# Linear attention and a snake MLP on one core: second products and attention rearranged in the first three tiles

## The chip, the core and the metric

The kernel runs on one NeuronCore of a Trainium2 chip. Five engines work side by side, each with its own queue of instructions taken in order: TensorE (PE, matrix products into the accumulation memory PSUM), VectorE (DVE), ScalarE (ACT), GpSimd (POOL) and SyncE (SP, which here issues the transfers). The metric is the device time of one execution in microseconds (us), as the median of several runs.

## The reference

```python
def _attn_ref(q, k, v):                 # 8 batches, 8 heads, 576 positions, 64 columns
    q_s = np.exp(q - max over the 64);  q_s = q_s / sum over the 64
    k_s = np.exp(k - max over the 576); k_s = k_s / sum over the 576
    kv = np.einsum('bhsd,bhse->bhde', k_s, v)
    return np.einsum('bhsd,bhde->bhse', q_s, kv)

def _moe_ref(x, w_in, w_out, alpha):    # x: 4608 x 512, w_in: 512 x 2048, w_out: 2048 x 512
    h = x @ w_in
    s = np.sin(alpha * h)
    g = h + s * s / (alpha + 1e-09)
    return g @ w_out
```

`x` is the attention's output with the heads side by side. All inputs and the output are float32.

## The kernel before

**Attention, per batch.** `load` brings q, k and v of one batch (1152 KB each) into staging buffers, six of which are shared with the weights (1 MB each). `exp_q` and `exp_k` take exponentials on ACT, in halves. `norm_q` sums q's exponentials over the 64 columns on DVE (L145), takes reciprocals (L146) and multiplies (L147) on the engines it is given. `cast_v` (L131) makes v bfloat16, beside a column of ones, so that the product of k and v (`kv_mm`, 36 small products into `kvp`, L156) also gives k's sums. `kv_norm` divides by these sums into `kvb` (L167, L168). `q_transpose` turns the normalised q in two groups (12 and 6 transposes into `tp`, L183) with a copy each to `qT` (L184). `attn_out` makes four groups of products `xp` (L196), each copied to `xT` (L199), the transposed bfloat16 input of the second part. All of this shares one PSUM buffer (`ps_a`, two banks), so each product waits for the copy before it.

**The MLP, in nine tiles of 512 rows.** A tile has 16 steps: `mm_h` makes 128 columns of h with four products of 512 columns (L209), `sine` takes the sine on ACT (L215) and squares it on ACT (L217), POOL (L219) or DVE (L221), `combine` makes one slice of g on DVE (L225). The string `SQ0` or `SQ1` says which engine squares in which step of tiles 0 and 1; later tiles square on ACT. The second product, `mm_o` (L229), takes 64 products per tile, 16 for each of four output blocks. `evac_o` (L234) copies a block out of PSUM into one of three buffers `o` and issues two transfers. h has four PSUM banks (`ps_h`), the blocks have two (`ps_o`).

**The order.** It is written out by hand: the order of the calls is the order on every engine. Batch 0's attention comes first, under transfers of the weights, which POOL casts to bfloat16 (L254, L257). Tile 0 then makes all of its h, then all four blocks of its second product at once (two in `ps_o`, two in `ps_h`), then attention 1 by itself. Tile t (from 1) makes its h with the second products of tile t-1 between its steps (none in tile 1), and holds attention t+1: the exponentials after step 0, kv at step 4, the transposes at 6 and 7, the products `xp` at 8 to 11. On SP's queue all transfers stand in the order of the calls.

ACT has one set of function tables active at a time: before an exponential that follows a sine, and a sine that follows an exponential, stands a table load.

Of the kernel before, what the change touches and what calls it, by code (L numbers as in the profile page):

```python
# [23 lines left out]
def kernel(  # L24
# [35 lines left out]
    spool = ctx.enter_context(tc.tile_pool(name="spool", bufs=3))  # L60
# [41 lines left out]
    def load_win(c):  # L102
        st = stage.tile([128, 4, 512], F32, name="st_w", tag="st")
        nc.sync.dma_start(out=st, in_=win_v[:, :, c * 512:(c + 1) * 512])
        wst["i", c] = st
# [55 lines left out]
    def kv_norm(b):  # L161
        A["kvb", b] = kt = att2.tile([128, 2, 2, D], BF16, name="kvb")
        kvr = small.tile([128, 2, 2], F32, name="kvr")
        for x in range(2):
            r = slice(64 * x, 64 * x + 64)
            src = A["kvp", b][r, :, 0:260].rearrange("p e (ii c) -> p e ii c", ii=2)
            nc.vector.reciprocal(kvr[r], src[:, :, :, x * 65 + 64])  # L167
            nc.vector.tensor_tensor(kt[r], src[:, :, :, x * 65:x * 65 + 64],  # L168
                                    kvr[r].unsqueeze(3).to_broadcast([64, 2, 2, D]), op=ALU.mult)
# [75 lines left out]
    load("v", v, 0, halves=True)  # L245
    for c in range(4):
        load_win(c)
    make_identity(nc, ident)
    DVE_CP(identb, ident)
    for n in range(2):  # L250
        nc.vector.memset(vb[n].rearrange("p j (i c) -> p j i c", i=4)[:, :, :, D:D + 1], 1.0)

    def cast_win(c, eng):
        eng(win[:, :, c * 512:(c + 1) * 512], wst["i", c])  # L254
# [4 lines left out]
    with tc.tile_pool(name="ps_s", bufs=4, space=PSUM) as ps_s:  # L259
# [16 lines left out]
        cast_win(0, POOL_CP)  # L276
# [3 lines left out]
        load_batch(1)  # L280
# [18 lines left out]
    combine(0, *pend)
    cast_wout(2, POOL_CP)  # L300
# [107 lines left out]
```

## Time and profile before

| | |
|---|---|
| median of three runs | 339.1 us (338.93 to 339.96) |
| the profiled execution | 340.48 us, its span 338.7 us |
| PE busy | 291.6 us (86%) |
| ACT busy | 237.5 us (70%) |
| DVE busy | 200.6 us (59%) |
| POOL busy | 71.7 us (21%) |

The span runs from the first to the last instruction that the profiler saw. A busy PE is not PE at its peak, since products overlap and their ends are modelled. The granted clock of TensorE is given as a share of full speed: 1.00 is 2.4 GHz, 0.50 is 1.2 GHz, and a number between is a mean over a stretch. The name in brackets behind an idle time is what ended it.

### The profile page before, as it was taken

The numbers are of one execution on the slowest core, as the hardware profiler recorded it, in microseconds if no ns is written. First come the engines' busy times: TensorE is split into PE (matmuls) and PEld (weight loads), VectorE is DVE, ScalarE is ACT, GpSimd is POOL, SyncE is SP. The second block draws the span as 40 slices with busy tenths as digits, with TensorE's granted clock in tenths as the row PEclk, the third lists the DMA queues.
The fourth block names the chain that finished last, engine by engine and source line by source line (L and its number), as shares of the span: only waits on it lengthen the run. The fifth ranks groups of instructions, "written<-read, shape, count | busy, mean of one in ns | idle before, by whom it ended". The sixth has DMA issues, their size and how long they took to land.

```text
span 338.7 us, 4528 instructions
## 1 busy us (share of the span) xinstructions
PE 291.6 (86%) x1713; PEld 134.9 (40%) x1713; DVE 200.6 (59%) x286; ACT 237.5 (70%) x328; POOL 71.7 (21%) x47
## 2 busy tenths in 40 slices
PE   0585895484799899989998999899989999999994
PEld 0432342322334444443444445444534444444441
DVE  3648761206886786487558755874687545555511
ACT  4476862268479867986897789778968777777600
POOL 0456632026443700150024003300400000000000
PEclk9979999556999999999999999999999999999999
DMA  7999903999500111850195029302111111211132
GB/s 266 389 386 387 391 10 76 309 392 391 215 0 0 33 31 33 297 199 19 38 333 173 3 62 362 120 4 59 33 31 31 32 31 33 50 44 33 32 93 62
DMA packets 22758, 46.44 MB, mean 137 GB/s; under 512 B 1728, under 2 KB 1744, under 8 KB 22736
## 3 DMA queue, kind: packets, MB, share of 16 engines
q1 hardware_dynamic: 22736, 46.15, 41.4%
q8 instruction: 13, 0.21, 0.3%
q14 instruction: 9, 0.07, 0.1%
HBM read 36.71 MB, written 9.44 MB: 136 GB/s over the span
## 4 chain that ended last, share of the span: by engine, by line
PE 49%; ACT 21%; DVE 18%; issue 6%; POOL 2%; DMA 2%; SPq 0%; ACTq 0%; POOLq 0%
PE op L229 22%; PE hp L209 20%; ACT s L215 7%; DVE g L225 7%; ACT ke L117 3%; ACT qe L117 3%; ACT L215 2%; ACT L117 2%; ACT s L217 2%; PE xp L196 2%; DVE kvb L168 2%; PE hp L229 2%; DVE s L221 2%; DVE qT L184 2%; PE tp L183 2%
## 5 line engine op out<-in xcount | busy, mean ns | idle before, releaser
L209 PE MATMUL hp<-xT,win 128*128 128x512 bf16 x576 | 150.5, 389 | 12.4 <-DVE g L225 11.4
L225 DVE SCALAR_TENSOR_TENSOR g<-s,inva_sb,hp 128x512 bf16<-128x512 f32 x144 | 105.9, 744 | 70.4 <-ACT s L217 65.2
L229 PE MATMUL op<-wout,g 128*128 128x512 bf16 x544 | 138.6, 380 | 0.0
L215 ACT ACTIVATE s<-hp,alpha_sb 128x512 f32<-128x512 f32 x144 | 97.8, 683 | 49.7 <-PE hp L209 36.8
L209 PEld LDWEIGHTS <-win 128*128 128x128 bf16 x576 | 56.8, 100 | 84.5 <-issue 21.4
L217 ACT ACTIVATE s<-s 128x512 f32<-128x512 f32 x126 | 79.4, 630 | 4.0
L229 PEld LDWEIGHTS <-g 128*128 128x128 bf16 x576 | 53.8, 98 | 63.4 <-issue 0.5
L147 POOL TENSOR_TENSOR qn<-qe,qs 128x2304 bf16<-128x2304 bf16 (+1 forms) x7 | 26.7, 3817 | 115.2 <-PE hp L209 100.7
L145 DVE TENSOR_REDUCE qs<-qe 128x36 f32<-128x2304 bf16 (+1 forms) x10 | 20.7, 2071 | 27.2 <-ACT qe L117 27.2
L234 DVE COPY o<-op 128x512 f32<-128x512 f32 x33 | 22.3, 676 | 14.0 <-PE op L229 14.0
L183 PE MATMUL tp<-identb,qn 128*128 128x128 bf16 x144 | 11.9, 234 | 20.9 <-DVE qn L147 9.2
L199 DVE CAST xT<-xp 128x512 bf16<-128x512 f32 (+1 forms) x28 | 20.8, 745 | 5.5 <-PE xp L196 5.5
L219 POOL TENSOR_TENSOR s<-s 128x512 f32<-128x512 f32 x12 | 12.9, 1076 | 39.4 <-ACT s L215 39.4
L183 PEld LDWEIGHTS <-qn 128*128 128x128 bf16 x144 | 9.8, 104 | 26.7 <-issue 16.3
L117 ACT ACTIVATE qe<-st_q 128x1152 bf16<-128x1152 f32 x16 | 17.8, 1156 | 3.4 <-DMA st_q<-in_q_dram 3.4
L131 POOL CAST vb<-st_v 128x1152 bf16<-128x1152 f32 x14 | 16.9, 1236 | 15.2 <-DMA st_v<-in_v_dram 15.2
L117 ACT ACTIVATE ke<-st_k 128x1152 bf16<-128x1152 f32 x16 | 17.7, 1149 | 0.7 <-DMA st_k<-in_k_dram 0.7
L196 PE MATMUL xp<-qT,kvb 64*64 64x256 bf16 (+1 forms) x128 | 10.4, 320 | 5.4 <-DVE kvb L168 2.5
L156 PE MATMUL kvp<-vb,ke 64*128 64x130 bf16 x288 | 12.4, 252 | 0.9 <-ACT qT L184 0.9
L156 PEld LDWEIGHTS <-ke 64*128 64x128 bf16 x288 | 10.8, 112 | 4.2 <-ACT s L215 3.0
L215 ACT ACT_TABLE_LOAD x8 | 10.3, 1283 | 1.7 <-PE hp L209 1.6
L117 ACT ACT_TABLE_LOAD x8 | 10.3, 1283 | 0.9 <-PEq L392 0.7
(28 smaller groups left out, 75.8 us busy)
## 6 DMA issues: line engine op xcount, KB each, us to landing
out_dram<-o SPq DMA_DIRECT2D x72, 128.0 KB, 2.4
st_q<-in_q_dram SPq DMA_DIRECT2D x7, 1152.0 KB, 6.3
st_k<-in_k_dram SPq DMA_DIRECT2D x7, 1152.0 KB, 9.6
st_v<-in_v_dram SPq DMA_DIRECT2D x7, 1152.0 KB, 11.1
st_w<-in_moe_w_in_dram SPq DMA_DIRECT2D x4, 1024.0 KB, 13.6
st_w<-in_moe_w_out_dram SPq DMA_DIRECT2D x4, 1024.0 KB, 15.7
st_q<-in_q_dram SPq DMA_DIRECT2D x2, 576.0 KB, 4.3
st_k<-in_k_dram SPq DMA_DIRECT2D x2, 576.0 KB, 6.4
```

Source lines behind the costliest of these rows:

```text
L117: nc.scalar.activation(dst[:, :, ii * 128:(ii + 1) * 128].rearrange("p j (x d) -> p x j d", x=2), src[:, ii::2], AX.Exp)
L145: nc.vector.tensor_reduce(part, src, axis=AXL.X, op=ALU.add)
L147: engs[h].tensor_tensor(dst, src, part.unsqueeze(3).to_broadcast([128, J, w, D]), op=ALU.mult)
L156: nc.tensor.matmul(kvp[:, e, ii * 130:(ii + 1) * 130], ke[r, j, ii * 128:(ii + 1) * 128], vt[r, j, ii * 130:(ii + 1) * 130], start=(j == 0 ...
L183: nc.tensor.transpose(tp[:, h, 2 * jj + ii], qn[:, j, ii * 128:(ii + 1) * 128], identb)
L199: eng(xT[:, ii::2, c0:c0 + n], xp[:, :, 0:n])
L209: nc.tensor.matmul(hp, win[:, ki, ni * 128:(ni + 1) * 128], xT[:, ki, t * MF:(t + 1) * MF], start=(ki == 0), stop=(ki == 3))
L215: nc.scalar.activation(s, hp, AX.Sin, scale=alpha_sb[:, ni:ni + 1])
L217: nc.scalar.activation(s, s, AX.Square)
L225: nc.vector.scalar_tensor_tensor(G[t][:, ni], in0=s, scalar=inva_sb[:, ni:ni + 1], in1=hp, op0=ALU.mult, op1=ALU.add)
L229: nc.tensor.matmul(acc, G[t][:, ni, j * 128:(j + 1) * 128], wout[:, ni, :], start=(ni == 0), stop=(ni == nN - 1))
L234: eng(o, acc)
```

## The change

The order of the first three tiles is rewritten.

- Front: the first half of q of batch 0 is normalised on POOL, v is cast on DVE, 14 products on data without use run on PE ahead of the transposes, a sine of one element loads its table ahead of tile 0, and the first quarter of w_in comes and is cast in two parts. All loads up to batch 2 are issued here, in the order weights, batch 1, batch 2; before, batch 2 came after tile 0's outputs.
- Tile 0: the squares go round ACT, DVE and POOL; h uses six PSUM banks (four of `ps_h` and two of `ps_o`); POOL's casts of the weights stand at other steps.
- Its second product is made in two pairs of blocks, with attention 1 between the products of the second pair.
- Tile 1 makes its h with no attention in it, then 50 of its 64 second products, with attention 2 between them. Tile 2 makes its h with the 14 products that are left and with attention 3 (exponentials after step 2, kv at step 7, the rest at 9 to 15), and squares on POOL and ACT in turn.
- From tile 3 on the order is as before, except that kv is at step 5, the transposes at 7 and 9, and `xp` at 10 to 13.
- `kv_norm` takes one reciprocal for both halves; the last evacuation is split over DVE and ACT, and its second transfer is issued on ACT's queue; the sines have four buffers instead of three.

```diff
-    spool = ctx.enter_context(tc.tile_pool(name="spool", bufs=3))
+    spool = ctx.enter_context(tc.tile_pool(name="spool", bufs=4))
...
-        kvr = small.tile([128, 2, 2], F32, name="kvr")
+        kvr = small.tile([128, 2, 2, 2], F32, name="kvr")
+        src = A["kvp", b][:, :, 0:260].rearrange("p e (ii x c) -> p e ii x c", ii=2, x=2)
+        nc.vector.reciprocal(kvr, src[:, :, :, :, D])
...
+        if wide and ni % 6 >= 4:
+            hp = ps_o.tile([128, MF], F32, name="op", tag="o")
+        else:
+            hp = ps_h.tile([128, MF], F32, name="hp", tag="h")
...
+        if last:
+            nc.vector.tensor_copy(o[:, 0:dm // 2], acc[:, 0:dm // 2])
+            nc.scalar.copy(o[:, dm // 2:], acc[:, dm // 2:])
+        else:
+            eng(o, acc)
...
+            q_eng = nc.scalar if last and hf else nc.sync
...
+    load_win(0, parts=2)
+    for c in range(1, 4):
+        load_win(c)
     for c in range(4):
-        load_win(c)
+        load_wout(c)
+    load("q", q, 1)
+    load("k", k, 1)
+    load("v", v, 1, halves=True)
+    load_batch(2)
...
-        norm_q(0, [V, V])
-        cast_v(0, [GP, V])
-        for c in range(4):
-            load_wout(c)
+
+        warm = ps_s.tile([128, 4, 128], F32, name="warm", tag="a")
+        for n in range(14):
+            nc.tensor.matmul(warm, identb, A["qe", 0][:, 0:4, 0:128], start=True, stop=True)
+        norm_q(0, [GP, V])
+        cast_v(0, [V, V])
         for g in range(2):
-            q_transpose(0, g, ps_s, ACT_CP)
+            q_transpose(0, g, ps_s, (ACT_CP, ACT_CP)[g])
+        nc.scalar.activation(zero, zero, AX.Sin)
...
+    SQ0 = "ADPADPADPADPADPA"
     for ni in range(nN):
+        h_slot(0, ni, SQ0[ni], lag, wide=True)
+        flush(lag, 1)
+        if ni in (0, 2, 5):
+            cast_win((0, 2, 5).index(ni) + 1, POOL_CP)
+        elif ni in (8, 11, 14):
+            cast_wout((8, 11, 14).index(ni), POOL_CP)
+    flush(lag, 0)
     cast_wout(3, POOL_CP)
...
+    def o_pair(t, j0, pool):
+        tag = "o" if pool is ps_o else "h"
+        accs = [pool.tile([128, dm], F32, name=tag + "p", tag=tag) for _ in range(2)]
+        for ni in range(nN):
+            for n in range(2):
+                mm_o(t, j0 + n, ni, accs[n])
+                yield
+        for n in range(2):
+            evac_o(t, j0 + n, accs[n], (DVE_CP, ACT_CP)[n])
+            if n == 0:
+                yield
...
     exp_q(1)
-    norm_q(1, [V, GP])
+    norm_q(1, [GP, V])
+    os = o_pair(0, 0, ps_o)
+    take(os)
     exp_k(1)
-    cast_v(1, [V, GP])
+    cast_v(1, [GP, V])
+    os = o_pair(0, 2, ps_h)
+    take(os, 16)
+    q_transpose(1, 0, ps_a, ACT_CP)
+    take(os, 2)
+    q_transpose(1, 1, ps_a, ACT_CP)
+    take(os, 2)
     kv_mm(1, 0, ps_a)
     kv_mm(1, 1, ps_a)
     kv_norm(1)
+    take(os, 6)
     for ii in range(2):
         attn_out(1, ii, 0, ps_a, DVE_CP)
+        take(os, 2)
         attn_out(1, ii, 1, ps_a, ACT_CP)
+        take(os, 1)
+    take(os)
+
+    SQ1 = "PAPDPAPAPPDPAPAP"
+    for ni in range(nN):
+        h_slot(1, ni, SQ1[ni], lag, wide=True)
+        flush(lag, 1)
+    flush(lag, 0)
...
+    attn_front(2, [V, GP])
+    os = o_stream(1)
+    take(os, 32)
+    kv_mm(2, 0, ps_a)
+    kv_mm(2, 1, ps_a)
+    kv_norm(2)
+    take(os, 4)
+    q_transpose(2, 0, ps_a, DVE_CP)
+    take(os, 3)
+    q_transpose(2, 1, ps_a, DVE_CP)
+    take(os, 3)
+    for n in range(4):
+        attn_out(2, n // 2, n % 2, ps_a, (DVE_CP, ACT_CP)[n % 2])
+        take(os, 2)
...
+    SQ2 = "PAPAPAPAPAPAPAPA"
+    for ni in range(nN):
+        hp = h_slot(2, ni, SQ2[ni], lag)
+        flush(lag, 1)
+        if ni == 2:
+            flush(lag, 0)
+            attn_front(3, [GP])
+            take(os)
+        attn_back(3, ni - 7)
+    flush(lag, 0)
+
+    for t in range(3, nT):
...
+            if b is not None:
+                attn_back(b, ni - 5)
```

`h_slot` calls `mm_h` and `sine` and puts the step on a list; `flush` calls `combine` for all but the given number of steps on the list. `take(os, n)` issues the next n second products. `attn_front` calls `exp_q`, `exp_k`, `cast_v`, `norm_q` and the next batch's loads; `attn_back(b, n)` does kv at n = 0, the transposes at 2 and 4, and one `attn_out` each at 5 to 8.

## Rows read from the trace of the kernel before

**Rows 1.** Table of stretches: us; busy us and instructions by engine, PEclk, DMA share, GB/s

```profile
54.50:70.24 15.74, 6.33 (x73) 4.00 (x72) 3.63 (x8) 4.67 (x6) 0.00 (x0) 0.60 0.86 269
70.24:98.56 28.32, 20.66 (x125) 9.14 (x125) 18.53 (x27) 18.66 (x23) 13.34 (x10) 0.80 0.71 264
...
131.40:164.20 32.80, 31.59 (x200) 14.52 (x199) 22.35 (x33) 27.34 (x39) 6.32 (x3) 1.00 0.43 141
```

**Rows 2.** The page, DMA traffic in 40 slices of 8.47 us

```profile
GB/s 266 389 386 387 391 10 76 309 392 391 215 0 0 33 31 33 297 199 19 38 333 173 3 62 362 120 4 59 33 31 31 32 31 33 50 44 33 32 93 62
```

**Rows 3.** Groups by line and shape: busy us, mean ns of one, idle before and releaser

```profile
L225 DVE SCALAR_TENSOR_TENSOR g<-s,inva_sb,hp 128x512 bf16<-128x512 f32 x144 | 105.9, 744 | 70.4 <-ACT s L217 65.2 <-POOL s L219 4.9
...
L215 ACT ACTIVATE s<-hp,alpha_sb 128x512 f32<-128x512 f32 x144 | 97.8, 683 | 49.7 <-PE hp L209 36.8 <-DVE g L225 8.8 <-DVE kvr L167 3.0
L217 ACT ACTIVATE s<-s 128x512 f32<-128x512 f32 x126 | 79.4, 630 | 4.0
...
L117 ACT ACTIVATE ke<-st_k 128x1152 bf16<-128x1152 f32 x16 | 17.7, 1149 | 0.7 <-DMA st_k<-in_k_dram 0.7
...
L219 POOL TENSOR_TENSOR s<-s 128x512 f32<-128x512 f32 x12 | 12.9, 1076 | 39.4 <-ACT s L215 39.4
...
L117 ACT ACT_TABLE_LOAD x8 | 10.3, 1283 | 0.9 <-PEq L392 0.7
...
L147 POOL TENSOR_TENSOR qn<-qe,qs 128x1152 bf16<-128x1152 bf16 x1 | 2.4, 2418 | 5.4 <-DVE qs L146 5.4
```

**Rows 4.** Timeline of the front and of tile 0: start us, us, engine, line, idle before

```profile
6.24 1.35 DVE L145 TENSOR_REDUCE qs<-qe 128x18 f32<-128x1152 bf16 x1 [2.96 <-ACT qe L117]
...
10.88 1.36 DVE L147 TENSOR_TENSOR qn<-qe,qs 128x1152 bf16<-128x1152 bf16 x1
...
14.22 2.13 PE L156 MATMUL kvp<-vb,ke 64*128 64x130 bf16 x36
...
18.97 0.38 PE L209 MATMUL hp<-xT,win 128*128 128x512 bf16 x1 [0.54 <-ACT xT L199]
...
20.83 0.69 ACT L215 ACTIVATE s<-hp,alpha_sb 128x512 f32<-128x512 f32 x1
...
30.71 1.89 POOL L257 CAST wout<-st_w 128x2048 bf16<-128x2048 f32 x1
...
31.94 1.21 DVE L221 TENSOR_TENSOR s<-s 128x512 f32<-128x512 f32 x1 [0.39 <-ACT s L215]
```

**Rows 5.** Timeline of attention 1 and the start of tile 1

```profile
58.54 1.45 ACT L184 COPY qT<-tp 128x1536 bf16<-128x1536 bf16 x1
...
70.24 5.63 PE L209 MATMUL hp<-xT,win 128*128 128x512 bf16 x15 [0.25 <-ACT xT L199]
...
80.89 1.86 PE L209 MATMUL hp<-xT,win 128*128 128x512 bf16 x4 [5.02 <-DVE g L225]
```

**Rows 6.** Timeline of the start of tile 2, and of tile 3

```profile
98.56 2.75 PE L209 MATMUL hp<-xT,win 128*128 128x512 bf16 x12 [0.48 <-DVE g L225]
...
133.48 1.03 PE L209 MATMUL hp<-xT,win 128*128 128x512 bf16 x4
...
135.14 1.11 SPq L237 DMA_DIRECT2D out_dram<-o  x2
...
143.93 1.20 PE L156 MATMUL kvp<-vb,ke 64*128 64x130 bf16 x36
...
144.22 0.75 DVE L225 SCALAR_TENSOR_TENSOR g<-s,inva_sb,hp 128x512 bf16<-128x512 f32 x1 [1.26 <-ACT s L217]
...
148.78 0.83 PE L183 MATMUL tp<-identb,qn 128*128 128x128 bf16 x12 [0.74 <-DVE kvb L168]
...
151.59 0.49 PE L183 MATMUL tp<-identb,qn 128*128 128x128 bf16 x6 [0.47 <-DVE qT L184]
```

**Rows 7.** Timeline of the end

```profile
319.09 14.84 PE L229 MATMUL op<-wout,g 128*128 128x512 bf16 x68
...
333.97 0.69 DVE L234 COPY o<-op 128x512 f32<-128x512 f32 x1 [2.76 <-PE op L229]
```

More of the change, by code (lines that the diff above doesn't have):

```diff
@@ L100, with load_win @@
     wst = {}
-    def load_win(c):
+    def load_win(c, parts=1):
         st = stage.tile([128, 4, 512], F32, name="st_w", tag="st")
-        nc.sync.dma_start(out=st, in_=win_v[:, :, c * 512:(c + 1) * 512])
+        n = 4 // parts
+        for h in range(parts):
+            nc.sync.dma_start(out=st[:, h * n:(h + 1) * n], in_=win_v[:, h * n:(h + 1) * n, c * 512:(c + 1) * 512])
         wst["i", c] = st
@@ L275 @@
         kv_norm(0)
-        cast_win(0, POOL_CP)
+        cast_win(0, POOL_CP, parts=2)
         for ii in range(2):
@@ L301, with h_slot, flush @@
-    cast_wout(3, POOL_CP)
-    accs = [ps_o.tile([128, dm], F32, name="op", tag="o") for _ in range(2)]
-    accs += [ps_h.tile([128, dm], F32, name="hp", tag="h") for _ in range(2)]
-    for ni in range(nN):
-        for j in range(4):
-            mm_o(0, j, ni, accs[j])
+    def h_slot(t, ni, sq, lag, wide=False):
+        hp = mm_h(t, ni, wide)
+        s = sine(t, ni, hp, sq)
+        lag.append((t, ni, hp, s))
+        return lag
+    def flush(lag, keep):
+        while len(lag) > keep:
+            combine(*lag.pop(0))
@@ new lines @@
+    lag = []
+    SQ0 = "ADPADPADPADPADPA"
+    for ni in range(nN):
+        h_slot(0, ni, SQ0[ni], lag, wide=True)
[5 more added lines that the diff above has]
+    flush(lag, 0)
+    cast_wout(3, POOL_CP)
+    def o_pair(t, j0, pool):
[9 more added lines that the diff above has]
+                yield
@@ L308, with take @@
+    def take(it, n=None):
+        for _ in iter(int, 1) if n is None else range(n):
+            if next(it, 0) == 0:
+                return
     exp_q(1)
-    norm_q(1, [V, GP])
+    norm_q(1, [GP, V])
+    os = o_pair(0, 0, ps_o)
+    take(os)
     exp_k(1)
-    cast_v(1, [V, GP])
-    for j in range(4):
-        evac_o(0, j, accs[j], ACT_CP if j % 2 else DVE_CP)
-    load_batch(2)
-    for g in range(2):
-        q_transpose(1, g, ps_a, ACT_CP)
+    cast_v(1, [GP, V])
+    os = o_pair(0, 2, ps_h)
@@ L330, in o_stream, with attn_front, attn_back @@
                 if ni == nN - 1:
-                    evac_o(t, j, acc, DVE_CP)
+                    evac_o(t, j, acc, DVE_CP, last=(t == nT - 1 and j == 3))
                 yield
-    SQ1 = "PAPDPAPDPAPDPAPA"
-    for t in range(1, nT):
+    def attn_front(b, engs):
+        exp_q(b)
+        exp_k(b)
+        cast_v(b, [GP, GP])
+        norm_q(b, engs)
+        if b + 1 < B:
+            load_batch(b + 1)
+    attn_front(2, [V, GP])
[12 more added lines that the diff above has]
+        take(os, 2)
+    def attn_back(b, n):
+        if n == 0:
+            kv_mm(b, 0, ps_a)
+            kv_mm(b, 1, ps_a)
+            kv_norm(b)
+        elif n in (2, 4):
+            q_transpose(b, n // 2 - 1, ps_a, DVE_CP)
+        elif 5 <= n < 9:
+            attn_out(b, (n - 5) // 2, (n - 5) % 2, ps_a, DVE_CP)
+    SQ2 = "PAPAPAPAPAPAPAPA"
[9 more added lines that the diff above has]
+    for t in range(3, nT):
         b = t + 1 if t + 1 < B else None
-        os = o_stream(t - 1) if t > 1 else None
+        os = o_stream(t - 1)
         done = 0
-        pend = None
         for ni in range(nN):
@@ L342 @@
             if b is not None:
[L343 to L377 removed]
+                attn_back(b, ni - 5)
+            s = sine(t, ni, hp, "A")
+            combine(t, ni, hp, s)
+            if b is not None and ni == 0:
+                attn_front(b, [GP])
+            want = 20 + 11 * ni // 4 if b is not None else 4 * (ni + 1)
+            take(os, min(64, want) - done)
+            done = min(64, want)
+        take(os)
+    take(o_stream(nT - 1))
 _INS = ['q', 'k', 'v', 'moe_w_in', 'moe_w_out', 'moe_alpha']
```

69 lines of the change are left out of this document (11 added, 58 removed).

## The prediction

> **What bounds the kernel now.** I read the table of stretches first, to see which engine is full where. In a middle tile (the stretch from 131.4 [rows 1]) PE is busy 31.59 of 32.80 us at full clock, ACT 27.34, DVE 22.35: PE sets the pace there. The start is different. From 54.5 to 70.24, where attention 1 runs alone, PE works 6.33 of 15.74 us at a granted clock of 0.60, and in tile 1 (70.24 to 98.56) 20.66 of 28.32 us at 0.80. So PE's holes lie before the third tile, and there the change is made. Next come the DMA traffic [rows 2], to see when loads can bind, and the groups by line and shape for the durations [rows 3]; then the timeline of the first tiles, for what ends each hole [rows 4, 5], of a middle tile [rows 6] and of the end [rows 7].
>
> The total number of big products does not change. What counts is the moment at which tile 3's first product starts (133.48 now [rows 6]), since from there on both programs do the same work, then what a middle tile takes, and the tail. A big product takes 14.84 us / 68 = 0.218 us at full clock [rows 7], so 32 take 7.0 us, and a step of four 0.87 us, with 1.03 from the first's start to the last's result (the one at 133.48 [rows 6]).
>
> **Front (batch 0).** The first half of norm_q goes to POOL (2.42 us for a half [rows 3]) instead of DVE (1.36 [rows 4]). DVE then reduces the second half 1.36 earlier, but its multiplication comes behind POOL's, so the transposes start only some 0.6 earlier. Fourteen new warm-up products lie ahead of them on PE. They start behind the first exponential, when DVE's first reduction does (6.24 [rows 4]), take 3.1 us at full clock and 6.1 at half, and cost nothing as long as they end before the normalised data are there, at about 11.6; at half clock throughout they would take back the 0.6. The small kv products took 2.13 us here against 1.20 in a middle tile [rows 4, 6]; at the higher clock they and the transposes should be some 1.8 us shorter. About 0.7 of this is taken up on ACT, whose first qT copy alone is 1.45 [rows 5]. I set the first product at 17.3 instead of 18.97, with bounds of 0 and 2.6 earlier. The table load of the sine (1.28 [rows 3]), which now lies between the first product and the first sine at 20.83 [rows 4], is done ahead on an idle ACT, so the first sine starts at 18.4. v's casts (both on DVE), w_in's first part in two loads and two casts, and one more buffer for s I cost at nothing: DVE waits for v's second half anyway, and POOL for w_in.
>
> **Tile 0.** Three steps now hold one square each on ACT, DVE and POOL, and one cast of 1.89 us follows on POOL. Per three steps ACT needs 3 x 0.683 + 0.63 = 2.7, DVE 3 x 0.744 + 0.55 = 2.8, POOL 1.08 + 1.89 = 3.0 us [rows 3, 4]. But a square on DVE waits for POOL: the one begun at 31.94 ended at 33.15, 0.55 after the cast that ran from 30.71 to 32.60 [rows 4]. If DVE goes first when a cast ends, POOL's next square starts 0.5 later, and three steps take 3.5. Five such periods, a start of some 1.5 and the lag of the last step put the last g 20.4 us behind the first product, at 37.7. If POOL were not held up it would be 5 x 0.5 = 2.5 earlier.
>
> The Trainium skill (GPSIMD Engine Reference, Specifications) states that POOL's SBUF interfaces are shared with VectorE and contend with DVE instructions that have two SBUF inputs. It speaks against five such squares among six casts; by it the period is 3.5, without it 3.0, and the trace agrees by the 0.55 above.
>
> The first pair of second products no longer waits for all of g: PE follows the g tiles and the w_out casts, and ends at about 41.3. Loads bind nothing: DMA moves 386 to 391 GB/s in the second to fifth slices, up to 42.3 [rows 2], batch 1 stands behind the weights in the same order on SP as now, and k and v (2.4 MB) are its last 6 us; so q is there at about 37. From there exponentials, two reductions and the half on POOL end at 43.3, and the transposes come 16 products into the second pair, at 44.8.
>
> Batch 2's loads now stand on SP's queue ahead of tile 0's outputs. They move 3.5 MB, 9 us at that rate, so the first outputs land at about 53. The fourth evacuation, at 55.5, needs the first's buffer (there are three); the cover is 2 us. If it goes, ACT's evacuation is late, and the sines of tile 1 behind it.
>
> **Attention 1.** Its chain over the single PSUM buffer of attention, from the first qT copy (58.54) to tile 1's first product (70.24), takes 11.7 us [rows 5]. It keeps its form: copy, transpose, copy, kv, kv_norm (one reciprocal less), four times product and copy. At full clock kv is 0.93 shorter, and by the same ratio I estimate 0.9 for the transposes and the xp products, 0.2 for the reciprocal: 9.7 us. The 16 remaining products of the pair fit into its waits. Behind 12 transposes of 0.83 in all [rows 6] it starts at 45.7, so tile 1 starts at 55.5 (at the low clock at 57.5) instead of 70.24. This is the largest step: 14.7 us up to here.
>
> **Tile 1** now holds no attention. ACT is its limit: result of the first product 1.06, table 1.28, 16 x 0.683 + 5 x 0.63 = 14.1: to 72.0 [rows 3]. POOL's nine squares (9.7) and DVE's 16 x 0.744 and two squares lie beside it. Then on ACT another table load and four exponentials of 1.15, 5.9 us, to 77.9; PE does 32 products of the second pass meanwhile (to 78). Beside it DVE reduces batch 2 in halves, the last ending near 79.1 with its reciprocal; behind it on DVE stand two evacuations (0.69 each [rows 7]) and kv_norm (1.1 estimated), so kv_norm ends at 81.5. The transposes, their copies and the four products and copies then take what attention 1's chain takes without kv and kv_norm, 9.7 - 1.2 - 0.9 = 7.6, with 18 second products in its waits: 89.1. There tile 2 starts.
>
> **Tile 2** is like tile 1 of before: exponentials within it, attention 3 at steps 7 to 15, PE idle behind the table loads as at 80.89, where it had been idle 5.0 us and four products then took 1.86, the lower of its two clocks [rows 5]. That tile took from 70.24 to 100.3 (the third of the products from 98.56 [rows 6]), 30.1 us. Against it ACT has three squares more (1.9, in PE's shadow), the 14 left products fit into the idle 5 us, and the last xT copy now falls behind the last step: 0.5. So 30.6, and tile 3 starts at 119.7 against 133.48: **13.8 us**. What is given back here of the 14.7 (and of the 50 products done ahead) is that tile 2 has no second products to fill its waits.
>
> **Tiles 3 to 6.** kv moves from step 4 to 5, the transposes from 6 and 7 to 7 and 9. The waits of 0.74 (kvb) and 0.47 (qT) at the transposes [rows 6], 1.21 per tile, go. But kv at 143.93 fills a wait: step 5 needs the bank that the g from 144.22 to 144.97 frees, and without kv PE would be there after three products, at 144.5. So 0.5 comes back: 0.7 per tile, **2.8 us** in four; bounds 0 and 4.8.
>
> **Tail.** The last copy (0.69 [rows 7]) is split over DVE and ACT: between 0 and half of it, 0.35, is gained; I take 0.3, as most of such a copy grows with its columns. One of the two last issues goes to ACT's queue, where the trace has none: between 0 and the 0.55 of one on SP (two in 1.11 [rows 6]); I take 0.3, in all **0.6 us**.
>
> **Sum.** 13.8 + 2.8 + 0.6 = 17.2. The profiled execution took 340.48 us around a span of 338.7, the runs shown have 339.1 as median; the span falls to 321.5 and the median to 339.1 - 17.2 = **321.9**.
>
> **Rivals.**
> *Attention 1 and 2 aren't hidden.* PE falls to 1.2 GHz in the stretches that mix them with second products (as at 54.5 to 70.24), the two chains take 2 us more each, and PE's products no longer fit into their waits, up to 4 us: 326 to 330. Against it: the lower clock came with holes of 5.0 us [rows 5] and a PE busy for 40% of a stretch [rows 1], and here I find holes of 1.5 and, worked out as above, 72% from 41.3 to 55.5 and 82% from there to 89.1.
> *Nothing gained in tiles 3 to 6*: another wait takes all of the 1.21: 324.7.
> *Cast and square run side by side in tile 0*, and POOL isn't held up: 2.5 less, 319.4. Against it stands the one square shown.
> *Slower than before*: PE stays at 1.2 GHz from tile 0's second products up to tile 3. From 41.3 to 119.7 it has 32 + 64 + 64 + 64 = 224 big products, 48.8 us; at half clock 48.8 more, of which its idle time there, some 18, hides part: 31 us late, 14 slower than before. It decides from about 0.72 of them at half clock. For it: 0.60 and 0.80 in the stretches of now; against it: the clock came back within tile 1 each time, as its mean of 0.80 shows.
> That the change does nothing can't be, as PE's instructions stand in another order.
>
> **How the numbers follow.** Forecast 0.47 (its own range 319.5 to 324), nothing in tiles 3 to 6 0.20, attention not hidden 0.17, POOL free 0.13, slower 0.03. The range from 317.5 (POOL free, and the most from tiles 3 to 6) to 328 (the middle of the rival with the lower clock) leaves out the rest of that rival and the slower case, under 2 in 10 with what else may be mis-sized. The runs shown spread over 0.3%, about what a measurement of this kernel can tell from no change. Faster 0.96, same 0.01, slower 0.03: only the last rival ends over 338.
>
> **What would show it.** First sine near 18.4 with no table load ahead of it; DVE squares in tile 0 ending 0.55 behind POOL's casts; the last g of tile 0 near 37.7; tile 1's first product near 55.5, tile 2's near 89, tile 3's near 120; a granted clock of 1.00 from 40 to 90; tiles 3 to 6 at 32.1 us each, with the wait at step 5 on g. Wrong would make it: a clock of 0.5 in the mixed stretches, evacuations that wait for output buffers, tile 2 over 33 us, or middle tiles still at 32.8.

## The result and the profile after

The changed kernel takes 320.99 us (median of four runs, 320.12 to 321.96) against 339.41 us (four runs, 338.93 to 339.96): a ratio of 0.9457, with a 95% interval of 0.9422 to 0.9493. The prediction was 321.9 us. The profiled execution took 321.48 us around a span of 319.7 us, so the span is 19.0 us shorter than before's 338.7; the medians differ by 18.4, and the sum of the prediction had 17.2.

The table of stretches of the changed kernel, with the same columns as [rows 1]. It is cut at the first products of tiles 0 to 3 (17.32, 57.17, 88.89 and 118.66) and at the last g of tile 0 (39.29); the last row is most of a middle tile (31.4 of its 31.8 us). In tiles 1 and 3 a single product runs ahead of the others, which wait for the last part of `xT`; the start is counted where the others run on (in tile 3, one product's 0.22 us before the three at 118.88).

```profile
17.32:39.29 21.97, 20.83 (x80) 8.47 (x80) 16.20 (x21) 16.16 (x24) 17.59 (x11) 0.86 1.05 388
39.29:57.17 17.88, 14.94 (x120) 7.22 (x119) 9.73 (x14) 7.95 (x10) 6.30 (x4) 1.00 0.82 304
57.17:88.89 31.72, 28.97 (x183) 13.43 (x183) 22.62 (x33) 21.38 (x30) 14.37 (x12) 1.00 0.46 145
88.89:118.66 29.77, 23.00 (x150) 10.73 (x149) 18.85 (x27) 23.85 (x32) 15.85 (x13) 0.94 0.74 256
...
121.09:152.50 31.41, 31.04 (x198) 14.43 (x197) 22.11 (x31) 26.92 (x38) 6.26 (x3) 1.00 0.11 26
```

The stretch that holds attention 1 (39.29 to 57.17) now has PE busy for 14.94 of 17.88 us at a granted clock of 1.00, where [rows 1] had 6.33 of 15.74 at 0.60; the stretch of tile 1 has 1.00 instead of 0.80. The lowest stretch is tile 0, with 0.86; in before it was 0.93 there (18.97 to 43.22).

The timeline of the changed kernel from the front to the end of tile 0 (start us, us, engine, line, idle before):

```profile
12.67 0.68 PE L158 MATMUL kvp<-vb,ke 64*128 64x130 bf16 x18
...
17.32 6.54 PE L215 MATMUL hp<-xT,win 128*128 128x512 bf16 x16 [1.18 <-ACT xT L201]
...
19.22 0.69 ACT L221 ACTIVATE s<-hp,alpha_sb 128x512 f32<-128x512 f32 x1 [1.95 <-PE hp L215]
...
27.67 1.89 POOL L276 CAST win<-st_w 128x2048 bf16<-128x2048 f32 x1
...
28.72 1.38 DVE L227 TENSOR_TENSOR s<-s 128x512 f32<-128x512 f32 x1
...
29.52 1.48 POOL L225 TENSOR_TENSOR s<-s 128x512 f32<-128x512 f32 x1
...
30.95 1.89 POOL L279 CAST wout<-st_w 128x2048 bf16<-128x2048 f32 x1
```

Against [rows 4], kv comes in halves of 0.68 us, the sine's table is loaded ahead, at 14.59, and the first product starts at 17.32 instead of 18.97. But its sixteen products take 6.54 us, where 16 at full clock take 3.5 [rows 7]. In steps of 2 us (the same columns as above):

```profile
14.00:16.00 2.00, 1.09 (x25) 0.56 (x19) 1.26 (x4) 1.97 (x4) 1.39 (x2) 1.00 1.05 406
16.00:18.00 2.00, 0.82 (x6) 0.35 (x3) 1.08 (x2) 1.27 (x3) 0.69 (x1) 0.61 1.05 390
18.00:20.00 2.00, 2.00 (x6) 0.73 (x5) 0.00 (x0) 0.75 (x2) 1.64 (x1) 0.50 1.05 389
...
24.00:26.00 2.00, 2.00 (x11) 0.89 (x10) 0.90 (x2) 1.97 (x4) 2.00 (x2) 1.00 1.05 389
```

The clock that had been 1.00 falls to its lower level (0.50, 1.2 GHz) between 16 and 18 us and is back at 1.00 by 24. In before the clock falls at tile 0's first big products too, but for half as long (0.59 from 20 to 21 us, 0.50 to 23, 0.71 to 24). The front won full clock for the small products and lost some 3 us more of it in tile 0.

The timeline of attention 1 and of the tiles behind it, beside [rows 5, 6]:

```profile
38.65 2.22 ACT L119 ACTIVATE qe<-st_q 128x1152 bf16<-128x1152 f32 x2 [0.54 <-DMA st_q<-in_q_dram]
...
46.46 0.83 PE L185 MATMUL tp<-identb,qn 128*128 128x128 bf16 x12
...
47.33 1.44 ACT L186 COPY qT<-tp 128x1536 bf16<-128x1536 bf16 x1 [1.42 <-PE tp L185]
...
57.17 3.18 PE L215 MATMUL hp<-xT,win 128*128 128x512 bf16 x14 [0.25 <-ACT xT L201]
...
57.62 1.28 ACT L221 ACT_TABLE_LOAD   x1
...
72.44 1.28 ACT L119 ACT_TABLE_LOAD   x1
...
102.21 1.87 PE L215 MATMUL hp<-xT,win 128*128 128x512 bf16 x4 [3.89 <-DVE g L231]
...
118.88 0.81 PE L215 MATMUL hp<-xT,win 128*128 128x512 bf16 x3 [1.22 <-DVE xT L201]
...
121.09 1.28 ACT L119 ACT_TABLE_LOAD   x1
...
152.90 1.28 ACT L119 ACT_TABLE_LOAD   x1
```

From the qT copy to tile 1's first product attention 1 takes 57.17 - 47.33 = 9.84 us, with 16 second products in it, instead of 11.7 with none. In before, the chain also started late, for a reason that the prediction names only as a risk of the changed kernel: the fourth block's copy on ACT, just ahead of the qT copy at 58.54 [rows 5], waited for an output transfer (there are three buffers `o`):

```profile
58.06 0.58 ACT L234 COPY o<-hp 128x512 f32<-128x512 f32 x1 [3.00 <-DMA out_dram<-o]
```

With the blocks in pairs the fourth copy comes at the end of attention 1 (57.01) and waits for no transfer. Tile 3's products run on from 118.66, against 133.48: 14.8 us. The exponentials' table loads of tiles 3 to 6 then come every 31.81 us; a middle tile of before took 32.80 [rows 1].

The groups of the middle tiles (121 to 249 us) show what is left of the waits of [rows 6]; the last columns are the idle time before the group and what ended it:

```profile
L215 PE MATMUL hp<-xT,win 128*128 128x512 bf16 x260 | 66.7, 379 | 1.5 <-DVE g L231 1.5
...
L185 PE MATMUL tp<-identb,qn 128*128 128x128 bf16 x72 | 5.3, 219 | 0.0
```

The transposes wait for nothing any more; the products of h wait 1.5 us for g in four tiles, 0.37 in each. The end, beside [rows 7]:

```profile
315.16 0.42 DVE L241 COPY o<-op 128x256 f32<-128x256 f32 x1 [2.76 <-PE op L235]
315.62 0.37 ACT L242 COPY o<-op 128x256 f32<-128x256 f32 x1 [13.79 <-DVE o L241]
...
316.02 0.56 ACTq L248 DMA_DIRECT2D out_dram<-o  x1
```

ACT's half of the last copy waits for DVE's half, and both issues, on SP's and on ACT's queue, begin at 316.02, 0.86 us after the first half began.

### The profile page after: what moved, and what is told of

Its sections match the earlier page's. It is cut to its first block, busy times and chain, and to the rows that moved or that the text cites. A ratio compares the mean times of both kernels' runs of the same rounds, so it can differ in the third digit from the quotient of the medians.

```text
span 319.7 us, 4552 instructions
## 1 busy us (share of the span) xinstructions
PE 290.9 (91%) x1727; PEld 133.9 (42%) x1727; DVE 197.6 (62%) x281; ACT 231.8 (72%) x321; POOL 82.8 (26%) x58
## 3 DMA queue, kind: packets, MB, share of 16 engines
HBM read 36.71 MB, written 9.44 MB: 144 GB/s over the span
## 4 chain that ended last, share of the span: by engine, by line
PE 54%; ACT 19%; DVE 13%; POOL 7%; issue 4%; DMA 1%; SPq 0%; ACTq 0%; POOLq 0%; DVEq 0%
PE hp L215 23%; PE op L235 23%; DVE g L231 6%; ACT s L221 5%; POOL s L225 3%; ACT qe L119 3%; ACT ke L119 3%; PE tp L185 3%; DVE qs L147 2%; ACT L119 2%; ACT L221 2%; PE xp L198 2%; PE kvp L158 2%; ACT s L223 2%; POOL wout L279 2%
## 5 line engine op out<-in xcount | busy, mean ns | idle before, releaser
L215 PE MATMUL hp<-xT,win 128*128 128x512 bf16 x544 | 140.0, 387 | 8.7 <-DVE g L231 5.9
L231 DVE SCALAR_TENSOR_TENSOR g<-s,inva_sb,hp 128x512 bf16<-128x512 f32 x136 | 100.2, 745 | 70.3 <-ACT s L223 56.1
L235 PE MATMUL op<-wout,g 128*128 128x512 bf16 x544 | 135.5, 379 | 1.7 <-DVE o L244 0.8
L221 ACT ACTIVATE s<-hp,alpha_sb 128x512 f32<-128x512 f32 x136 | 92.2, 683 | 39.2 <-PE hp L215 35.0
L223 ACT ACTIVATE s<-s 128x512 f32<-128x512 f32 x115 | 72.4, 630 | 3.7
L225 POOL TENSOR_TENSOR s<-s 128x512 f32<-128x512 f32 x22 | 25.0, 1144 | 38.4 <-ACT s L221 38.3
L147 DVE TENSOR_REDUCE qs<-qe 128x18 f32<-128x1152 bf16 (+1 forms) x11 | 20.8, 1887 | 17.2 <-ACT qe L119 17.2
L201 ACT CAST xT<-xp 128x640 bf16<-128x640 f32 x6 | 4.0, 690 | 15.4 <-PE xp L198 15.4
L198 PEld LDWEIGHTS <-kvb 64*64 64x64 bf16 x128 | 4.7, 103 | 15.8 <-issue 13.9
L158 PE MATMUL kvp<-vb,ke 64*128 64x130 bf16 x288 | 10.3, 223 | 0.7 <-ACT qT L186 0.5
```

The source lines that it names most:

```text
L147: nc.vector.tensor_reduce(part, src, axis=AXL.X, op=ALU.add)
L201: eng(xT[:, ii::2, c0:c0 + n], xp[:, :, 0:n])
L215: nc.tensor.matmul(hp, win[:, ki, ni * 128:(ni + 1) * 128], xT[:, ki, t * MF:(t + 1) * MF], start=(ki == 0), stop=(ki == 3))
L221: nc.scalar.activation(s, hp, AX.Sin, scale=alpha_sb[:, ni:ni + 1])
L223: nc.scalar.activation(s, s, AX.Square)
L225: nc.gpsimd.tensor_tensor(s, s, s, op=ALU.mult)
```

## The experiments

All are the changed kernel with one edit, unless said otherwise. The question behind them: my theory was that the gain is attention 1 behind second products, the steps of the middle tiles, and a tile 0 that the squares pace; the rivals were that the clock alone does it (any order that keeps PE at 2.4 GHz would be as good), and that transfers set the start of attention 1 whatever tile 0 does.

**Attention 1 by itself.** The second pair's 32 products come first, attention 1 after them with no second product between its parts.

```diff
-    take(os, 16)
+    take(os, 32)
     q_transpose(1, 0, ps_a, ACT_CP)
-    take(os, 2)
     q_transpose(1, 1, ps_a, ACT_CP)
...
```

> Attention 1 comes behind all second products of tile 0 again, nothing stands between its steps. Theory A (its waits hide the second products): the 16 products of the second pair, 0.216 us each, come out of hiding, so tile 1's first product starts 3.5 us later than 57.2 and the whole is 3 to 3.5 us slower than the changed kernel (about 324.3). Theory B (what it gains is PE's clock): with nothing between its steps PE falls to 1.2 GHz as in the kernel before, the chain from the first qT copy to tile 1's first product takes 11.7 us instead of 9.8, tile 1 starts slowly: 5.5 us slower or more (about 326.5).

Measured: 327.28 us (325.55 to 329.25), ratio 0.9635 (0.9586 to 0.9684): 6.3 us more than the changed kernel by the medians. The profiled execution is the slowest of the four (329.25), its span 7.7 us longer than the changed kernel's. One row of the timeline and one of the table of stretches:

```profile
53.88 2.13 PE L158 MATMUL kvp<-vb,ke 64*128 64x130 bf16 x36 [0.89 <-ACT qT L186]
...
62.21 2.29 PE L215 MATMUL hp<-xT,win 128*128 128x512 bf16 x5 [0.25 <-ACT xT L201]
```

```profile
50.00:62.21 12.21, 5.96 (x73) 3.62 (x72) 3.03 (x6) 3.67 (x5) 0.00 (x0) 0.65 0.28 102
62.21:70.00 7.79, 7.79 (x25) 3.05 (x25) 2.68 (x4) 5.96 (x9) 2.35 (x3) 0.68 0.88 261
```

Tile 1 starts 5.0 us later: 3.45 for the 16 products that no longer lie in the waits, the rest for a chain of 11.2 us instead of 9.84, with kv back at the 2.13 of [rows 4]. Then tile 1 starts at a clock of 0.68, and from its sine's table load (62.67) to tile 3's table load (128.84) it takes 66.2 us instead of 63.5: 2.7 more. Theory B, with the clock, is right, and its price (5.5 us or more) fits the 6.3. In this execution 4.1 of the 7.7 us, 1.4 in the chain and 2.7 behind it, go with the lower clock; taking the 3.45 from the 6.3, it is 2.8 by the medians: about half either way. Of the 1.4, kv's 0.93 is seen to be the clock's; the rest was not separated. A run with products without use in attention 1's waits, which would hold the clock up and hide nothing, was not made.

**Tiles 1 and 2 in the order of before**, behind the new tile 0 and attention 1 (so without the six banks in tile 1).

```diff
+    SQ1 = "PAPDPAPDPAPDPAPA"
+    for t in (1, 2):
+        b = t + 1
+        os = o_stream(1) if t == 2 else None
...
+            hp = mm_h(t, ni)
+            if ni == 4:
+                kv_mm(b, 0, ps_a)
+                kv_mm(b, 1, ps_a)
+                kv_norm(b)
+            elif ni in (6, 7):
+                q_transpose(b, ni - 6, ps_a, DVE_CP)
+            elif 8 <= ni < 12:
+                attn_out(b, (ni - 8) // 2, ni % 2, ps_a, DVE_CP)
```

> Tiles 1 and 2 in the order of before (attention 2 inside tile 1's first products, all 64 second products of tile 1 and attention 3 inside tile 2), front, tile 0 and tiles from 3 on as changed. Theory A (the two traces subtracted: 13.1 us are gained up to tile 1's start, 14.8 up to tile 3's): 1.7 us slower than the changed kernel, about 322.7. Rival B (tile 1 of before was slow only because PE came out of attention 1 at 1.2 GHz): no difference within 0.5 us, about 321. Rival C (the new tiles 1 and 2 carry more than the subtraction shows, since tile 1 has six banks and no exponentials): 3 us slower or more.

Measured: 321.01 us (320.40 to 322.19), ratio 0.9453 (0.9418 to 0.9487): no difference. The two table loads on ACT that frame tiles 1 and 2, and the wait in tile 1:

```profile
56.40 1.28 ACT L221 ACT_TABLE_LOAD   x1
...
120.21 1.28 ACT L119 ACT_TABLE_LOAD   x1
```

```profile
65.53 1.86 PE L215 MATMUL hp<-xT,win 128*128 128x512 bf16 x4 [6.19 <-DVE g L231]
```

The two tiles take 63.81 us this way and 63.47 (57.62 to 121.09) in the changed kernel: the whole new order of tiles 1 and 2, six banks included, is worth 0.3 us in these two executions once attention 1 hands PE over at full clock, and nothing by the medians. Counted from tile 1's first product, the stretch is 65.67 in before (70.24 to 135.91), 64.26 here (55.95 to 120.21) and 63.92 in the changed kernel (57.17 to 121.09). The second step, 0.3, is the order. The first, 1.4, is not simply the clock: 1.07 of it lies ahead of the first sine, which comes 2.82 us behind the first product in before and 1.75 here. In before the sine's table load stood behind the wait for the product's result:

```profile
71.76 1.28 ACT L215 ACT_TABLE_LOAD   x1 [1.57 <-PE hp L209]
```

In the first experiment, at a clock of 0.68, the load came ahead of the result (62.67) and the sine 1.76 us behind the product, so the low clock alone doesn't bring this back. Tile 1 alone still has its idle time behind the tables, 6.19 us, and the lower clock after it (1.86 for four products). Rival B's time is right here; its reason, that tile 1 was slow only by the clock, isn't shown.

**The middle tiles' steps of before**: kv at 4, transposes at 6 and 7, `xp` from 8.

```diff
-                attn_back(b, ni - 5)
+                if ni == 4:
+                    attn_back(b, 0)
+                elif ni in (6, 7):
+                    attn_back(b, 2 * (ni - 5))
+                elif 8 <= ni < 12:
+                    attn_back(b, ni - 3)
```

> From tile 3 on kv at step 4, transposes at 6 and 7, products xp at 8 to 11, as before the change; all else as changed. Theory A (the 1.0 us per middle tile comes from the steps alone): the period goes from 31.81 back to 32.8 us, 4.0 us slower in four tiles, about 325. Rival B (a part is from kv_norm's missing reciprocal, 0.22 us in the wait for kvb): period 32.45, 2.5 us slower, about 323.5. Rival C (the fourth buffer of the sines): steps change nothing, period 31.8.

Measured: 324.55 us (323.62 to 324.81), ratio 0.9548 (0.9518 to 0.9578). A middle tile takes 32.66 us, 0.85 more (the first of them starts 0.5 earlier than in the changed kernel's execution, at 120.59). The transposes over four tiles, in the groups:

```profile
L185 PE MATMUL tp<-identb,qn 128*128 128x128 bf16 x72 | 5.3, 219 | 4.2 <-DVE kvb L170 2.2 <-DVE qT L186 2.0
```

So 3.4 us of the 4.0 gained in tiles 3 to 6 come from the steps, nearer to theory A than to B. The kvb wait is 0.55 per tile here and was 0.74 in [rows 6], with the same steps: the other 0.15 per tile probably come with `kv_norm`'s single reciprocal, which I had counted in attention 1 alone. Neither it nor the fourth buffer of the sines was taken back by itself.

**kv at step 4, the transposes at 7 and 9.**

```diff
-                attn_back(b, ni - 5)
+                if ni == 4:
+                    attn_back(b, 0)
+                elif ni > 5:
+                    attn_back(b, ni - 5)
```

> From tile 3 on kv goes back to step 4, the transposes stay at 7 and 9, xp at 10 to 13. Theory A (kv at step 5 leaves the wait of 0.37 us on g at step 5's first product, and kv at step 4 fills it): period 31.4 instead of 31.8 us, 1.5 us faster than the changed kernel, about 319.5. Rival B (the wait only moves, to kv or to a later step): same as the changed kernel, 321.

Measured: 318.94 us (317.82 to 319.31), ratio 0.9382 (0.9344 to 0.9420): better than both kernels. The products of h of its middle tiles, in the groups over 121 to 249 us:

```profile
L215 PE MATMUL hp<-xT,win 128*128 128x512 bf16 x267 | 68.6, 379 | 0.0
```

The 1.5 us of waiting for g are gone, and the transposes wait for nothing either. A middle tile takes 31.27 us, 0.54 less: 2.1 in four, as the medians differ. The wait for g at step 5 was the hole that kv had filled; the change took kv out of it. Theory A is right; of the 2.1 us, the 0.6 above the 1.5 show in no wait of these groups.

**No warm-up products in the front.**

```diff
-        warm = ps_s.tile([128, 4, 128], F32, name="warm", tag="a")
-        for n in range(14):
-            nc.tensor.matmul(warm, identb, A["qe", 0][:, 0:4, 0:128], start=True, stop=True)
```

> The 14 products without use at the front are left out. Theory A (they bring PE to 2.4 GHz for the transposes and kv of batch 0, and that is what brings tile 0 forward): kv takes 2.1 us instead of 1.4, the transposes 2.0 instead of 1.1, tile 0's first product comes 1 to 1.5 us later than 17.3 to 17.9, the whole is 1 to 1.5 us slower than the changed kernel (about 322.2). Rival B (ACT's copies and the landing of w_in set tile 0's start): no difference, 321.

Measured: 321.08 us (320.92 to 321.39), ratio 0.9465 (0.9451 to 0.9479): no difference. The first rows are of the timeline, the last one of the table of stretches:

```profile
11.55 1.99 PE L185 MATMUL tp<-identb,qn 128*128 128x128 bf16 x17 [0.93 <-DVE qn L149]
13.48 1.82 PE L158 MATMUL kvp<-vb,ke 64*128 64x130 bf16 x36
...
19.80 0.69 ACT L221 ACTIVATE s<-hp,alpha_sb 128x512 f32<-128x512 f32 x1 [1.53 <-PE hp L215]
```

```profile
22.00:24.00 2.00, 2.00 (x11) 0.88 (x9) 1.77 (x3) 1.49 (x3) 0.70 (x1) 1.00 1.05 381
```

The transposes and kv are slow again, and the first sine is 0.6 us later; but the clock, which falls here too, is back at 1.00 by 22 us, and tile 0's last work on ACT ends, by the next table load, at 36.71 instead of 36.82. What the warm-up gives ahead of tile 0 is lost within it in these two executions: without it the lower clock lasts from 18 us to before 22, with it from 16 to beyond 22. Rival B's time is right, but not its reason: tile 0's first product did come 0.41 us later (17.73).

**More products without use**, four behind kv and six behind the last `xp`, so that PE stays busy up to tile 0.

```diff
             kv_mm(0, ii, ps_s)
+        warm2 = ps_s.tile([128, 4, 128], F32, name="warm2", tag="a")
+        for n in range(4):
+            nc.tensor.matmul(warm2, identb, A["qe", 0][:, 0:4, 0:128], start=True, stop=True)
...
+        for n in range(6):
+            nc.tensor.matmul(warm2, identb, A["qe", 0][:, 0:4, 0:128], start=True, stop=True)
```

> Ten more products without use: four between kv and xp of batch 0, six between xp and tile 0's first product, where PE was idle for 0.75 and 1.18 us. Theory A (the clock falls in these holes in most executions, and tile 0's first sines then come 1.7 us apart instead of 0.7 to 1.3): granted clock 1.00 from 12 us on, time from tile 0's first product to ACT's first exponential of batch 1 some 17.1 us instead of 18.5 to 19.5, the whole 1 to 1.5 us faster than the changed kernel (about 319.7); q of batch 1, which lands at 38, takes up the rest. Rival B (tile 0 is paced by POOL whatever the clock): no difference. Rival C (the products delay xp and the first product): 0.3 us slower.

Measured: 320.44 us (320.00 to 320.78), ratio 0.9444 (0.9430 to 0.9459). The timeline:

```profile
38.62 2.22 ACT L119 ACTIVATE qe<-st_q 128x1152 bf16<-128x1152 f32 x2 [2.31 <-DMA st_q<-in_q_dram]
```

The clock is 1.00 from the front to tile 1, and the table load behind tile 0 comes 1.8 us earlier, at 35.03; then ACT waits 2.31 us for q of batch 1. Tile 1's first product comes at 55.71 instead of 57.17, and this execution's span is 1.5 us shorter, as theory A has it; the medians differ by 0.5 us, hardly more than their intervals. PE is now free for the transposes when q is normalised (45.05), where in the changed kernel it was busy until 46.46. So the transfer of q is what comes next behind tile 0.

**Tile 0 without DVE's squares.** This kernel leaves out the five squares that DVE makes in tile 0, so those steps use the sine unsquared.

```diff
-        else:
+        elif t > 0:
             nc.vector.tensor_tensor(s, s, s, op=ALU.mult)
```

> Leaves out the five squares on DVE in tile 0 (these steps take the sine unsquared). Theory A (a square on DVE and POOL's work exclude each other, so three steps take 3.28 us): POOL's squares take 1.04 again instead of 1.48, three steps take 2.95, the last g of tile 0 comes 1.5 us earlier; q of batch 1, landing at 38, lets through about 1 us, about 320. Rival B (three steps are paced by ACT, or by PSUM banks): period 3.28, no difference, 321.

Measured: 320.79 us (320.17 to 321.18), ratio 0.9454 (0.9440 to 0.9468). The timeline:

```profile
30.45 1.89 POOL L279 CAST wout<-st_w 128x2048 bf16<-128x2048 f32 x1
...
32.30 1.04 POOL L225 TENSOR_TENSOR s<-s 128x512 f32<-128x512 f32 x1
33.29 1.89 POOL L279 CAST wout<-st_w 128x2048 bf16<-128x2048 f32 x1
...
38.62 2.22 ACT L119 ACTIVATE qe<-st_q 128x1152 bf16<-128x1152 f32 x2 [4.58 <-DMA st_q<-in_q_dram]
```

POOL's square is 1.04 us again instead of 1.48, and three steps take 2.84 us instead of 3.28, as theory A on the exclusion has it. The table load behind tile 0 comes 4.1 us earlier, at 32.75 (in an execution whose clock stayed at 1.00 in tile 0, which is part of it), and little of it arrives: ACT waits 4.58 us for q, which lands at 38.62 as in the run before, and tile 1's first product comes at 56.54, 0.6 earlier. In attention 1 the clock was lower here (0.70 from 46 to 48 us, 0.50 to 50).

**Four banks for h in tiles 0 and 1.**

```diff
-        h_slot(0, ni, SQ0[ni], lag, wide=True)
+        h_slot(0, ni, SQ0[ni], lag)
...
-        h_slot(1, ni, SQ1[ni], lag, wide=True)
+        h_slot(1, ni, SQ1[ni], lag)
```

> Tiles 0 and 1 make h in the four banks of before instead of six. Theory A (a step holds its bank for some 5 us from its first product to its g, so four banks allow one step in 1.25 us and six one in 0.8): tile 0 takes 1.2 us per step as before the change and gets 2 us longer, tile 1 gets 1 us longer, the whole is 2 to 3 us slower, about 323.5. Rival B (the order of the squares alone made tile 0 shorter): no difference, 321.

Measured: 324.78 us (324.53 to 324.95), ratio 0.9572 (0.9556 to 0.9587): 3.8 us more. One row of tile 0 from the timeline, and ACT's table loads around tile 1:

```profile
27.31 2.75 PE L215 MATMUL hp<-xT,win 128*128 128x512 bf16 x12 [1.06 <-DVE g L231]
...
58.24 1.28 ACT L221 ACT_TABLE_LOAD   x1
75.51 1.28 ACT L119 ACT_TABLE_LOAD   x1
```

Tile 0 now has four waits for g, 2.65 us together; with six banks both tiles have 0.5. Tile 1 takes 17.27 us between the loads instead of 14.82 (57.62 to 72.44). Theory A's total is right, its split is not: of tile 0's delay 0.6 us is left at tile 1's table load (58.24 against 57.62), and 2.45 us fall in tile 1: with no other work between its steps, four banks let the lag of a combine reach PE and so ACT. The 0.3 us that the new order of tiles 1 and 2 gains therefore hang on the six banks.

**q of batch 1 ahead of the last quarter of w_out**, with the late products of the kernel before last, and 10, 6 and 4 second products around the transposes instead of 16, 2 and 2.

```diff
-    for c in range(4):
+    for c in range(3):
         load_wout(c)
     load("q", q, 1)
+    load_wout(3)
...
-    take(os, 16)
+    take(os, 10)
     q_transpose(1, 0, ps_a, ACT_CP)
-    take(os, 2)
+    take(os, 6)
     q_transpose(1, 1, ps_a, ACT_CP)
-    take(os, 2)
+    take(os, 4)
```

> The ten later products without use of e6, and beside them: q of batch 1 loads ahead of the last part of w_out, and 10 second products instead of 16 stand before attention 1's transposes, the six others in its waits. Theory A (with tile 0 faster, attention 1 waits for the landing of q at 38.6): q lands at about 36, the normalised q is ready at 42.5 instead of 45.0, tile 1's first product comes at 54 instead of 55.7 in e6, the whole is 1.5 us faster than e6, about 318.8. Rival B (PE's products and the casts of w_out set the time): same as e6, 320.4.

Measured: 320.00 us (319.67 to 320.49), ratio 0.9429 (0.9405 to 0.9453). The timeline:

```profile
38.84 1.89 POOL L280 CAST wout<-st_w 128x2048 bf16<-128x2048 f32 x1 [0.62 <-DMA st_w<-in_moe_w_out_dram]
...
40.70 2.13 POOL L149 TENSOR_TENSOR qn<-qe,qs 128x1152 bf16<-128x1152 bf16 x1
...
41.33 2.70 DVE L149 TENSOR_TENSOR qn<-qe,qs 128x1152 bf16<-128x1152 bf16 x1
```

Against the kernel with late products, the exponentials start 1.7 us earlier (36.94) with no wait, but the transposes only 0.4 (44.67 against 45.05), and the medians differ by 0.4 with intervals that overlap. The wait has moved to POOL: the last cast waits for its weights, q's half on POOL stands behind the cast, and DVE's half then takes 2.70 us beside it. Theory A's size was wrong: mostly what rival B said. With both loads needed at the same time, changing their order moves the wait and doesn't remove it.

**That kernel with kv at step 4, and the last copy in one piece on DVE** (the two issues stay on SP's and ACT's queues).

```diff
-        if last:
-            nc.vector.tensor_copy(o[:, 0:dm // 2], acc[:, 0:dm // 2])
-            nc.scalar.copy(o[:, dm // 2:], acc[:, dm // 2:])
-        else:
-            eng(o, acc)
+        eng(o, acc)
...
+                if ni == 4:
+                    attn_back(b, 0)
+                elif ni > 5:
+                    attn_back(b, ni - 5)
```

> e9 with kv at step 4 in the tiles from 3 on (e4), and with the last evacuation as one copy on DVE, its two transfers still issued on SP and ACT. If the gains add up: 2.1 us for the step of kv in four tiles, 0.1 to 0.2 for the tail (the two half copies ran one after the other, 0.42 and 0.37, against 0.69 for one): 2.2 us faster than e9, about 316.5. If they don't (the middle tiles start with ACT further behind): 1 us or less.

Measured: 317.91 us (317.16 to 318.86, six runs), ratio 0.9367 (0.9344 to 0.9391), the lowest. The end of its timeline:

```profile
311.79 0.69 DVE L240 COPY o<-op 128x512 f32<-128x512 f32 x1 [2.76 <-PE op L235]
312.51 0.56 ACTq L244 DMA_DIRECT2D out_dram<-o  x1
```

2.1 us below the kernel before it; the middle tiles take 31.28 us as in the run with kv at step 4, and the issue follows the copy's start by 0.72 us instead of 0.86. The gains add, but beside that run (318.94) the intervals overlap.

## Why the prediction was right, point by point

The total was right, 0.9 us from the median. That it came so near is in part luck: up to tile 1 and in the tail the terms were 2.0 us too big (1.6 and 0.4), in tiles 1 and 2 and in tiles 3 to 6 they were 3.8 too small (2.6 and 1.2).

- **Up to tile 1's first product: 14.7 us predicted, 13.1 measured.** The front's first product was right (17.3 and 17.32; 17.29 to 17.94 in the six runs with the same front). The first sine was 0.8 late, and tile 0's last g came at 39.29 instead of 37.7. The mis-sized term is the start of tile 0: I had its products at full clock, and they ran at the lower one for about 6 us. Where the clock stayed at 1.00 (the profiled execution with tiles 1 and 2 in the old order), the last g came 19.5 us behind the first product instead of 22.0, and tile 1 started at 55.95, near my 55.5. The period of three steps was 3.28 us, where I had 3.5; against 2.84 without DVE's squares, the exclusion costs 0.44 a period and not 0.5. In the sum for DVE I took the 0.55 for a square; that is only what it overran the cast by, and a square alone takes 0.69 (at 21.65), which doesn't change which engine is the limit.
- **"Loads bind nothing" held, but only just.** q of batch 1 landed at 38.62, not 37. ACT waited 0.54 us for it, and this cost nothing: q was normalised at 45.01, and the transposes stood behind PE's products until 46.46. Where tile 0 ends earlier, the transfer does hold attention 1 (2.31 and 4.58 us of wait in two runs), and at most 1.5 us of a faster tile 0 reach tile 1. The 1.6 us come from my reading of [rows 2], which counts back from the end of the traffic: a landing comes later. In before q landed no earlier (issued at 25.86, 12.8 us to landing), and v at 44.6 (issued at 32.63, 12.0 us), when the traffic had already fallen to 187 GB/s from 42 to 43 us and 25 from 43 to 44.
- **Attention 1: 9.7 us predicted, 9.84 measured**, at a clock of 1.00. The rival in which it is not hidden, or runs at the lower clock, is what the first experiment brought about, and its 327.28 us lie in the 326 to 330 that I gave it.
- **Tiles 1 and 2: 0.9 us given back by the prediction, 1.7 gained.** Tile 1 took 31.7 us instead of 33.6. I had put the sine's table load behind the first product's result, where before had it (71.76); it ran ahead of it, at 57.62, 0.45 after the product's start, and the first sine came 0.6 sooner. The sines and squares took 13.5 us instead of 14.1. The tail of exponentials and attention 2 was 0.65 shorter (72.44 to 88.89). Tile 2 took 29.8 instead of 30.6. Of the 1.7 gained, 0.3 is the order, by the second experiment; of the other 1.4, 1.07 lies ahead of tile 1's first sine, and the clock's share was not separated.
- **Tiles 3 to 6: 2.8 predicted, 4.0 measured.** Both waits at the transposes went, and a wait came back at step 5, 0.37 us instead of 0.5. The rest, 0.15 a tile, probably goes with the single reciprocal, which no run took back. That nothing is gained here, the second rival, is out: the old steps alone cost 3.4 us.
- **Tail: 0.6 predicted, 0.2 measured.** Half a copy is shorter, as I had it, but the halves run one after the other.
- **POOL's squares free of DVE's, the third rival**, is out by 3.28 against 2.84 us. The Trainium skill (SBUF — State Buffer, SBUF: two separate sides) has it that a DVE instruction with two SBUF inputs and a GpSimd instruction that reads SBUF lock each other out for a whole instruction. The trace agrees, both ways: DVE's square at 28.72 ends 0.54 after the cast (29.56), and POOL's next one, at 29.52, ends 0.90 after DVE's (30.10); alone they take 0.69 and 1.04, so most of each comes after the other's end.
- **Slower than before** would have needed the lower clock from 41 us to tile 3; it was 1.00 from 39.29 to 88.89 and 0.94 in tile 2.

The terms sum to 14.8 + 4.0 + 0.2 = 19.0. Of the profiled span, taking one part back costs 7.7 us (attention 1 by itself), 3.3 (four banks) and 2.9 (the old steps); by the medians it is 6.3, 3.8 and 3.6. So the largest term is only in part what my theory says: of the 13.1 us up to tile 1, attention 1 among second products is worth 5.0 (62.21 against 57.17), and tile 1 starts 8.0 earlier than in before even without that (62.21 against 70.24). In those 8.0, 4.6 lie ahead of the transposes (50.14 against 54.70), from the front, tile 0 and the pairs together, and 3.0 are the wait for the output buffer; the front alone and the squares of tile 0 alone were not taken back, nor were the pairs of blocks.

## What to carry to other kernels

Put independent products into the waits of a serial chain: besides their own time they kept TensorE's clock up here, and about half of what hiding attention 1 gave went with the clock, in the chain and in the tiles behind it. Before moving work out of a wait, look at what that work was filling: the new steps closed two waits and, with kv at step 5, opened one; kv at step 4 with the late transposes closes all three. And when a stage gets faster, look at the next thing that it waits for: of four microseconds won in tile 0, most ended in a wait for q.

## What the hardware showed that was not expected

- The clock fell between 16 and 17 us (0.72 in that stretch, 0.50 in the next), though PE's longest idle time from 12 us up to then was 0.75 us; of the 1.18 us ahead of tile 0's first product, most came after the fall. From 14 to 16 us PE was busy for 1.09 of 2 us. It does not fall in each execution: of the same front and tile 0, one profiled execution (tiles 1 and 2 in the old order) kept 1.00 from 16 us on, and its tile 0 took 17.06 us from first product to table load, where the changed kernel's took 19.50. Those 2.4 us may be why runs of the changed kernel spread from 320.1 to 322.0: the two faster ones have a mean clock of 0.991 and 0.987, the two slower ones 0.984 each. That was not tested.
- In before, PE was idle for 5.02 us in tile 1 and came back at 1.86 us for four products [rows 5]; in the changed kernel 3.89 us did the same in tile 2 (1.87): the wait behind the tables has moved to tile 2. The lower clock behind it costs nothing there: without the warm-up products PE came back from the same wait at full clock, and from tile 2's first product to tile 3's table load both executions take 32.20 us (88.78 to 120.98, and 88.89 to 121.09). The row of the run without warm-up products:

```profile
102.09 1.02 PE L215 MATMUL hp<-xT,win 128*128 128x512 bf16 x4 [3.88 <-DVE g L231]
```
